# Last block's gate logits formed early, and the rows of the two last blocks placed by one-hot products

## The chip, the cores and the metric

One core of a Trainium2 chip runs the whole program. The metric is the device time of one execution in microseconds (us). Engines are named as in the profile: PE (TensorE, matrix products), PEld (its weight loads), DVE (VectorE), ACT (ScalarE), POOL (GpSimd) and SP (SyncE, which issues most DMAs).

## The reference, cut to what matters

```python
# 1. gated linear attention, step by step over 768 tokens, 2 batches x 8 heads x 40
m_new = max(f_t + m, i_t);  C = exp(f_t + m - m_new) * C + exp(i_t - m_new) * outer(v_t, k_t)
y_t = sigmoid(o_t) * (C @ q_t) / max(abs(n @ q_t), 1)
x = y as [1536, 320]
# 2. a dense layer pair, 2048 features
g = softplus(x @ w_in);   x2 = g @ w_out
# 3. eight experts, the best one for each token
logits = x2 @ w_gate;     e = argmax(logits);   p = softmax(logits)[e]
out = p * sigmoid(x2 @ w_output_gate)[e] * (relu(x2 @ w1[e]) @ w2[e])
```

Everything is float32. Where a product has to be exact enough for the argmax, an operand is split in a rounded high part and the rest (`xh`/`xl`, `gh`/`gl`, `part` 0 and 1), and several products are added.

## The kernel before

The 1536 tokens are six blocks of 256 (two tiles of 128, `t` = 0 and 1). Attention runs chunk by chunk (`chunk`, six chunks of 128 for both batches), and block `c` of stage 2 can begin when chunk `c` of both batches is done.

Stage 2: `up1` makes `ph`, the products of feature tile `f` (16 of them) with a block, eight 256-column products each. `softplus` (line 1188) turns `ph` into `g`: three ACT passes over `ab`, a DVE pass that writes `g`, an ACT copy `gh`, a DVE subtraction `gl`. `down1` (line 1239) adds `gh`, `gl` times `w_out` into `acc`. The features come in legs (0 to 4, 4 to 8, 8 to 16); the sum of a leg that isn't the last is kept in `row` by `keep_part`, and the last leg's sum is added to it by `take_row`.

Routing: when a block's last `acc` is full, `take_row` (line 874) writes `row`, turns it on PE (`x2tp`), copies it (`x2T`) and multiplies by `wg`, which holds both gates (`lg`). `route` finds the expert of each token (a DVE chain that ends in the one-hot `ohb`), PE counts how many tokens of an expert stand ahead (products with `tri` and `ones`), and a second DVE chain works out each token's place (`pos`). `scatter` sends the rows to the DRAM table `rows` by indirect DMAs from POOL. Stage 3 works on 15 slots of 128 places, each of one expert. The first four slots (`EARLY`) are needed at once, so `early_turn` (line 1124) builds their turned rows `xe` on PE: it transposes what blocks 0 to 4 have put there (`er`, read back from `rows`), and adds block 5's rows by products of `part` with `S`, the one-hot matrix of the places. `early_x` splits `xe` into the high and low half in `flat`, and the products `ph<-w1s,flat` of stage 3 begin.

Order: `Weaver` plans the program before it runs. Each engine has one queue that is worked off in the order in which the planner wrote it; the planner picks the next step by the start that its own price list gives, and by rank. A step that is priced too cheaply stands in the queue all the same, and what is behind it waits. `constants` (line 840) clears the routing tables on POOL and sends `wg` and the clearing of `rows` (19 DMAs); it comes up when 2, and then 12, up products are planned. `heat` (line 382) keeps PE busy until the gates have come in. `warm` (line 1151, called at 1477 to 1480) puts 14 idle products of 512 columns between the steps of the change-over to stage 3.

```python
W.add(warm(known, 5), 0)
W.add(warm(turned_rows[0], 2), 0)
W.add(warm(have_last_lg, 2), 0)
W.add(warm(have_turned, 5), 0)
```

Nearly all instructions of the trace have the line of a helper (L196), so steps are found by the names of their tiles.

Of the kernel before, what the change touches and what calls it, by code (L numbers as in the profile page):

```python
# [22 lines left out]
HEAT = 50  # L23
EARLY = 4
P = 128
# [209 lines left out]
def mlstm_moe_kernel(ctx: ExitStack, tc: tile.TileContext, q_t, k_t, k, v, i_gate, f_gate, o_gate,  # L235
# [16 lines left out]
    TPB = B  # L252
# [95 lines left out]
    scratch_all = moe.tile([P, (3 + NSP) * P + P // 2], F32, tag="row2", name="scratch")  # L348
    after_t = scratch_all[:, (3 + NSP) * P:].bitcast(BF16)
# [32 lines left out]
    def heat():  # L382
        warm, ev = yield from bank.get([P, 2 * P], F32, "heat")
        W.clock["P"] = 1.1
        yield "P"
        for _ in range(HEAT):
            PE.matmul(warm, ones, ones.unsqueeze(1).to_broadcast([P, 2, P]), start=True, stop=True)
        W.clock["P"] = 8.1
        W.signal(ev)

    def gates(n, c0, c1):
# [397 lines left out]
    def conv():  # L789
        for n in range(NF):  # L790
# [3 lines left out]
            t, e2 = yield from flt_ring.get([P, HIGH], U32, "wta", users=2)  # L794
# [8 lines left out]
            W.add(after(W.cur.out, low_p(t, e2, n)), 2)  # L803

# [6 lines left out]
    def low_p(t, ev, n):  # L811
        yield "G"
        psub(place(n)[64:P, 0:P], t[64:P, 0:P], place(n)[64:P, 0:P].bitcast(F32))
        W.signal(ev)
        W.signal(have_w[n])

# [23 lines left out]
    def constants():  # L840
        yield 2.0
# [17 lines left out]
        yield 12.0  # L859
# [14 lines left out]
    def take_row(row, t, acc, ev, part, xT, xT_ev, lg, lg_ev, eng, last):  # L874
        if part is not None:
# [5 lines left out]
            if last:  # L881
                W.add(after(W.cur.out, parts_of(row, t)), 2)
        else:
            yield eng
            copy(row[:, t, 0:DM], acc)
            copy(row[:, t, DM:CCOL], acc[:, 256:DM])
        W.signal(ev)
        xp, ev = yield from bank.get([P, 3, P], F32, "x2tp")
# [3 lines left out]
        if last:  # L892
            turned_rows[t].t = W.cur.out
        yield eng
        copy(xT, xp)
        W.signal(ev)
        if last:
            yield [turned_rows[TPB - 1]]
# [6 lines left out]
    def route(blk, acc, full, part):  # L905
# [9 lines left out]
        yield [full[0]]  # L915
        lg, ev = yield from bank.get([P, 64], F32, "lg")
        have_lg = Event(n=TPB)
        for t in range(TPB):
            xT, xT_ev = yield from xT_ring.get([P, 3, P], F32, "x2T")
            W.add(after(full[t], take_row(row, t, *acc[t], part, xT, xT_ev, lg, have_lg,  # L920
                                         "AV"[t % 2] if blk == NBLK - 1 else "A", blk == NBLK - 1)), 1)
        yield [have_lg]
# [10 lines left out]
        final = blk == NBLK - 1  # L933
        counts, counts_ev = (yield from bank_y.get([P, 64], F32, "counts")) if final else (lg, None)
        lgv = lg[:, 0:2 * T8].rearrange("p (t c) -> p t c", t=T2)
        le, lo_ = lgv[:, :, 0:E], lgv[:, :, E:2 * E]
        rank = counts[:, 2 * T8:3 * T8].rearrange("p (t e) -> p t e", e=E)
        tot = counts[:, 3 * T8:3 * T8 + E]
# [11 lines left out]
        tt(ohb, over(iota8, T2), bc(idx, E), ALU.is_equal)  # L950
        yield "P"
# [8 lines left out]
        yield "V"  # L960
        DVE.tensor_scalar(out=nmx, in0=mx, scalar1=-1.0, scalar2=None, op0=ALU.mult)
        tt(sel, lo_, ohb, ALU.mult)
        yield "V"
        DVE.tensor_reduce(out=oge, in_=sel, axis=AX.X, op=ALU.add)
        yield "A"
        for t in range(T2):
            ACT.activation(out=ex[:, t], in_=le[:, t], func=AF.Exp, bias=nmx[:, t:t + 1], accum_out=ssum[:, t:t + 1])
        ACT.activation(out=ef, in_=oge, func=AF.Exp, scale=-1.0)
        if final:
            W.signal(have_exps)  # L970
        yield [Event(ranked), state[blk], have_rows]
        if final:
            yield from place_last(small, tot, rank, ohb, ef, ssum, row, row_ev, ev, counts_ev, small_ev, blk)
            return
# [5 lines left out]
        yield from pause(blk)  # L980
# [21 lines left out]
        yield from pause(blk)  # L1002
        tt(t8, an, dn, ALU.mult)
        tt(c1, csi, rem.to_broadcast([P, E]), ALU.is_le)
        tt(room, room, tot, ALU.subtract)
        tt(c2, an, bn, ALU.add)
        yield from pause(blk)
        tt(nxt, nxt, t8, ALU.add)
        DVE.tensor_reduce(out=nmx[:, 0:1], in_=c1, axis=AX.X, op=ALU.add)
        tt(nmx[:, 1:2], total, rem, ALU.is_gt)  # L1010
        DVE.scalar_tensor_tensor(out=room, in0=c2, scalar=float(P), in1=room, op0=ALU.mult, op1=ALU.add)
        DVE.scalar_tensor_tensor(out=s128, in0=total, scalar=float(P), in1=s128, op0=ALU.mult, op1=ALU.add)
        yield from pause(blk)
        tt(nxt, nxt, tot, ALU.add)
        DVE.scalar_tensor_tensor(out=nmx[:, 1:2], in0=rem, scalar=0.0, in1=nmx[:, 1:2], op0=ALU.is_ge, op1=ALU.mult)
        W.signal(ev)
        yield from pause(blk)
        DVE.scalar_tensor_tensor(out=base, in0=room, scalar=s128, in1=nxt, op0=ALU.subtract, op1=ALU.add)
        DVE.scalar_tensor_tensor(out=esl, in0=nmx[:, 0:1], scalar=nmx[:, 1:2], in1=esl, op0=ALU.mult, op1=ALU.add)
        tt(rem, rem, total, ALU.subtract)  # L1020
        W.signal(small_ev)
        W.signal(state[blk + 1])
# [5 lines left out]
    def place_last(small, tot, rank, ohb, ef, ssum, row, row_ev, ev, counts_ev, small_ev, blk):  # L1028
# [17 lines left out]
        DVE.tensor_scalar(out=ef, in0=ef, scalar1=1.0, scalar2=None, op0=ALU.add)  # L1046
        yield "V"
        tt(m, m, over(dn, T2), ALU.mult)
        DVE.scalar_tensor_tensor(out=ef, in0=ssum, scalar=1e-9, in1=ef, op0=ALU.add, op1=ALU.mult)
        yield "V"  # L1050
        tt(nr, nr, m, ALU.add)
        DVE.reciprocal(out=row[:, :, CCOL], in_=ef)
# [8 lines left out]
        for t in range(T2):  # L1061
            W.add(after(placed, scatter(blk * TPB + t, row[:, t, :], posi[:, t:t + 1], row_ev)), 0)
        for t in range(T2):
            yield "V"
            DVE.tensor_scalar(out=chosen["S"][:, t], in0=chosen["iota"], scalar1=pos[:, t:t + 1], scalar2=None,
                              op0=ALU.is_equal)
        W.signal(have_chosen)
# [9 lines left out]
        for e in (ev, counts_ev, small_ev, state[blk + 1]):  # L1077
            W.signal(e)

    have_room, up_done, have_turned, have_exps, known = (Event() for _ in range(5))  # L1080
    have_last_lg, have_counts, have_chosen, have_parts, have_early = Event(), Event(), Event(), Event(n=TPB), Event()
    scattered_most = Event(n=NTILE - TPB)
    chosen, later = {}, {}
    x_done = Event(n=3)
# [12 lines left out]
    def early_rows():  # L1097
        yield [state[NBLK - 2]]
        for part in range(2):
            chosen["part", part], chosen["part_ev", part] = yield from row_ring.get([P, TPB, CCOL], F32R, "part")  # L1100
        W.signal(have_room)
# [4 lines left out]
        for n in range(EARLY // 2):  # L1106
            chosen["er", n], chosen["er_ev", n] = yield from raw_ring.get([P, 2, CCOL], F32, "er")
        chosen["S"], chosen["S_ev"] = yield from raw_ring.get([P, TPB, EARLY * P], F32R, "S")
# [6 lines left out]
    def parts_of(row, t):  # L1115
        yield [have_room]
# [657 lines left out]
```

## Time and profile before

| | |
|---|---|
| median of 3 runs | 435.1 us (434.52 to 436.67) |
| profiled execution | 435.17 us, of which 433.5 us are the span of the trace |
| PE busy | 410.1 us (95%), 3078 matrix products |
| DVE busy | 343.5 us (79%) |
| ACT busy | 302.5 us (70%) |
| POOL busy | 181.0 us (42%) |
| mean granted PE clock | 0.987 of full speed |

The span has three parts: attention, with stage 2 beginning among it, to about 130 us; stage 2 alone to about 278 us; stage 3 from about 294 us on. Between the last two stands the change-over. A busy share says how full an engine is over a stretch; what a stretch costs is read from the idle time of PE there and from the engine that ended it.

### The profile page before, as it was taken

Reading aid. Unit: us, or ns where it says so; the run is one execution under the profiler, and the core shown is the slowest. Engines: PE = TensorE matmul, PEld = TensorE weight load, DVE = VectorE, ACT = ScalarE, POOL = GpSimd, SP = SyncE. Lnnn points to the kernel's source line nnn. Section 1 sums busy time; section 2 is a strip of 40 time slices with the busy share of each in tenths; the row PEclk is TensorE's granted clock in tenths of the full one; section 3 lists DMA queues with packets and bytes.
Section 4 is the critical chain, followed back from the end, with each engine's and each line's share of the span. In section 5 each row is a group of like instructions: output and inputs, shape, how many; then the busy total and the mean of one; then the engine's idle time right before and its main releaser. Section 6 shows DMA issues by size and latency. Waiting matters only on the chain. (4 is left out here: it accounts for less than half of the span.)

```text
span 433.5 us, 9833 instructions
## 1 busy us (share of the span) xinstructions
PE 410.1 (95%) x3078; PEld 390.5 (90%) x3078; DVE 343.5 (79%) x904; ACT 302.5 (70%) x879; POOL 181.0 (42%) x246
## 2 busy tenths in 40 slices
PE   8877999999899999999999999899999999999994
PEld 6767999999899999999999999767998998998893
DVE  4999798998999999997657675666755898798663
ACT  2776699996868877777769669466798666566230
POOL 4256756756120111120201102127676287387654
PEclk9999899999999999999999999989999999999998
DMA  8958789499226412032101100128645636544112
GB/s 263 312 175 247 240 240 300 136 332 297 77 102 252 170 69 67 33 91 62 38 2 38 38 2 37 38 102 271 228 132 185 220 132 216 189 144 139 42 67 80
DMA packets 32284, 62.90 MB, mean 145 GB/s; under 512 B 4218, under 2 KB 16765, under 8 KB 32230
## 3 DMA queue, kind: packets, MB, share of 16 engines
q1 hardware_dynamic: 30742, 57.87, 41.0%
q0 software_dynamic: 1488, 4.35, 2.7%
q8 instruction: 28, 0.46, 0.4%
q14 instruction: 26, 0.21, 0.2%
HBM read 54.05 MB, written 8.65 MB: 145 GB/s over the span
## 5 line engine op out<-in xcount | busy, mean ns | idle before, releaser
L196 ACT ACTIVATE ab<-ab 128x256 f32<-128x256 f32 x192 | 77.4, 416 | 2.8
L196 PE MATMUL ph<-w1s,flat 128*128 x312 | 58.8, 332 | 2.6 <-DVE hr L196 1.5
L196 POOL TENSOR_TENSOR w1s<-w1raw,w1s 64x256 fp32r<-64x256 f32 (+1 forms) x39 | 39.4, 1027 | 48.5 <-ACT w1s L196 25.0
L196 PE MATMUL acc<-win,gh 128*128 128x320 f32 x240 | 56.1, 320 | 0.0
L196 DVE SCALAR_TENSOR_TENSOR g<-ph,ab 128x256 f32<-128x256 f32 x96 | 39.9, 419 | 20.2 <-ACT ab L196 19.5
L196 PE MATMUL yp<-w2s,hh 128*128 x240 | 54.6, 315 | 1.0 <-POOL w2s L196 0.9
L196 ACT ACTIVATE ab<-ph 128x256 f32<-128x256 f32 x96 | 36.0, 379 | 26.4 <-PE ph L196 26.2
L196 PEld LDWEIGHTS ph<-w1s,flat 128*128 128x128 f32 x312 | 46.6, 189 | 7.9 <-DVE hr L196 1.9
L196 DVE TENSOR_TENSOR gl<-g,gh 128x256 fp32r<-128x256 f32 x96 | 42.5, 447 | 7.9 <-ACT gh L196 7.2
L196 POOL DMA_INDIRECT rows<-row,rsm x12 | 12.0, 1004 | 80.4 <-DVE rsm L196 47.6
L196 POOL TENSOR_TENSOR w2s<-w2raw,w2s 128x640 fp32r<-128x640 f32 x22 | 39.1, 1808 | 8.7 <-issue 4.9
L196 ACT CAST gh<-g 128x256 fp32r<-128x256 f32 x96 | 38.1, 398 | 6.6 <-DVE g L196 4.7
L196 PEld LDWEIGHTS yp<-w2s,hh 128*128 128x128 f32 x240 | 39.8, 188 | 3.1 <-POOL w2s L196 1.1
L196 PE MATMUL ph<-win 128*128 128x256 f32 x250 | 40.8, 286 | 0.0
L196 DVE TENSOR_TENSOR hr<-ph,hr 128x256 f32<-128x256 f32 x60 | 24.7, 420 | 20.3 <-ACT hr L196 17.2
L196 PEld LDWEIGHTS acc<-win,gh 128*128 128x128 f32 x240 | 39.4, 191 | 0.0
L196 ACT COPY hr<-ph 128x256 f32<-128x256 f32 x60 | 22.6, 376 | 21.3 <-PE ph L196 19.2
L196 PE MATMUL acc<-win,gl 128*128 128x320 f32 x120 | 37.4, 312 | 0.0
L196 PE MATMUL yp<-w2s,hl 128*128 x120 | 37.2, 310 | 0.0
L196 PEld LDWEIGHTS ph<-win 128*128 128x128 f32 x250 | 34.3, 190 | 0.0
L196 PE MATMUL acc<-wou,gh 128*128 128x320 f32 x144 | 33.1, 315 | 1.2 <-ACT gh L196 1.2
L196 ACT CAST w2s<-w2raw 128x640 fp32r<-128x640 f32 x32 | 22.6, 735 | 13.9 <-PE yp L196 13.9
(209 smaller groups left out, 1070.6 us busy)
## 6 DMA issues: line engine op xcount, KB each, us to landing
w1raw<-in_w_dram SPq DMA_DIRECT2D x32, 384.0 KB, 4.4
wra<-in_w_in_dram SPq DMA_DIRECT2D x16, 704.0 KB, 5.1
w2raw<-in_w_dram SPq DMA_DIRECT2D x32, 320.0 KB, 3.2
abc<-abc_dram SPq DMA_DIRECT2D x4, 1024.0 KB, 7.8
rows<-pad SPq DMA_DIRECT2D x19, 194.0 KB, 4.4
qT<-in_q_t_dram SPq DMA_DIRECT2D x6, 512.0 KB, 4.4
kn<-in_k_dram SPq DMA_DIRECT2D x5, 416.0 KB
vn<-in_v_dram SPq DMA_DIRECT2D x6, 320.0 KB, 5.6
```

The lines of the kernel that those rows point to most:

```text
L196: return fn(*args, **kw)
```

## The change

- `heat` has 44 products in place of 50. The subtraction `ig - mm` on DVE is gone: PE adds minus `mm` to the turned `ig` by a product with a negative identity (`minus`).
- `constants` comes up at 20 and 26 planned up products in place of 2 and 12.
- The last block's last leg is cut in two: features 8 to 13, and 14 and 15 (`TAIL`). After the first of these the kept `row` is turned and multiplied by `wg` (`first_logits`, `part_logits`). For the two last features `vg` = `w_out` times `wg` is made once (`last_gates`), and the missing logits are `g` times `vg`, four products of 16 columns into the same `lg`. The `row` itself is finished later (`last_row`), behind the one-hot.
- Rows of block 4, too, are placed by one-hot products, so the read of `er` waits for blocks 0 to 3 alone. `xe` lies otherwise in its three banks: two banks hold two slots of two thirds each, one holds the last third of four slots. All products of high parts come ahead of those of low parts. A block takes 16 products of 256 columns and 4 of 512 (before: 12 of 512).
- The four calls of `warm` are gone. Scatters of the last block wait for the finished `row` and its weight.

```diff
-HEAT = 50
+HEAT = 44
+TAIL = 2
...
-        yield "V"
-        DVE.tensor_tensor(out=ig[:, t0:t1], in0=ig[:, t0:t1], in1=mm[:, t0:t1], op=ALU.subtract)
...
-            PE.transpose(gps[:, 1, c, :], ig[0:G, c * P:(c + 1) * P], ident[:G, :G])
+            PE.matmul(gps[:, 1, c, :], ig[0:G, c * P:(c + 1) * P], ident[:G, :G], start=True, stop=False, is_transpose=True)
+            PE.matmul(gps[:, 1, c, :], mm[0:G, c * P:(c + 1) * P], minus, start=False, stop=True)
...
+    def last_gates(t, ev, i):
...
+            PE.transpose(xp[0:n, kk, :], t[:, 3 * P + kk * P:3 * P + kk * P + n], ident)
...
+            PE.matmul(ps_, xT[0:n, kk, :], wg[0:n, kk, :], start=kk == 0, stop=kk == 2)
...
+        DVE.tensor_copy(out=vg[:, i], in_=ps_)
...
     def constants():
-        yield 2.0
+        yield 20.0
...
-        yield 12.0
+        yield 26.0
...
+    def first_logits(row, added):
+        yield [have_const, have_vg]
+        last["lg"] = lg, _ = yield from bank.get([P, 64], F32, "lg")
+        for t in range(TPB):
+            W.add(after(added[t], part_logits(row, t, lg)), 0.9)
+        yield [lg_parts, last_g]
+        for i in range(TAIL):
+            g, g_ev = last["g", i]
+            yield "P"
+            for t in range(TPB):
+                PE.matmul(lg[:, 2 * E * t:2 * E * (t + 1)], g[:, t * P:(t + 1) * P], vg[:, i], start=False,
+                          stop=t == TPB - 1 and i == TAIL - 1)
...
+    def last_row(row, t, acc, ev):
+        yield [turned_rows[t], have_ohb]
+        yield "V"
+        DVE.tensor_tensor(out=row[:, t, 0:DM], in0=acc, in1=row[:, t, 0:DM], op=ALU.add)
...
     def early_turn():
+        yield [have_early, known]
+        xe, half = [], EARLY // 2 * P
+        pieces = [[(0, 0, 2), (1, 0, 2)], [(2, 0, 4)], [(0, 2, 2), (1, 2, 2)]]
...
+        yield [have_chosen[LATE[0]], have_parts[LATE[0]]]
+        for n, group in enumerate(pieces):
+            for i in range(len(group)):
+                for part in range(2):
+                    for t in range(TPB):
+                        yield "P"
+                        product(n, i, LATE[0], t, part)
...
+        yield [have_chosen[LATE[1]], have_parts[LATE[1]]]
+        for part in range(2):
+            for n, group in enumerate(pieces):
...
+                        product(n, i, LATE[1], t, part, part == 1 and t == TPB - 1 and i == len(group) - 1)
...
+    legs[-1:] = [(NBLK - 1, cuts[-2], NF - TAIL), (NBLK - 1, NF - TAIL, NF)]
...
-    W.add(warm(known, 5), 0)
-    W.add(warm(turned_rows[0], 2), 0)
-    W.add(warm(have_last_lg, 2), 0)
-    W.add(warm(have_turned, 5), 0)
```

The planner writes another order from these. On POOL, in the attention part, the clearing of the routing tables stands before ahead of the product `v` that a chunk's state update (`kv` on PE) needs (`cst` is the state, `y` the chunk's result):

```order
L196 TENSOR_TENSOR cst_111<-cst_111,sm 40x4x41 x2
L196 MEMSET tri 128x128
L196 AFFINE_SELECT tri<-tri 128x128
L196 IOTA iota_115 128x8
L196 IOTA tokid 128x12
L196 MEMSET pad 128x388
...
L196 IOTA rem 128x1
L196 TENSOR_TENSOR v_575<-v_378,sm 128x328
```

and now:

```order
L197 TENSOR_TENSOR wou<-wta,wou 64x128 x2
L197 TENSOR_TENSOR y<-num,y 128x320
L197 MEMSET tri 128x128
L197 AFFINE_SELECT tri<-tri 128x128
L197 IOTA iota_120 128x8
...
L197 IOTA rem 128x1
L197 TENSOR_TENSOR y<-num,y 128x320
```

The fifteen small steps have moved from between the chunks to a place ahead of the last chunk's last result.

On PE, from the last up product of stage 2 to the places of the last block, the order before is this (`acc` are the last down products, `counts` the counting of tokens):

```order
L196 MATMUL ph<-xl,wou 128x256 x3
...
L196 MATMUL warm<-ones 128x512
L196 MATMUL acc_4141<-wou,gh 128x320 x2
...
L196 MATMUL x2tp<-ident,row 128x128 x3
L196 MATMUL lg<-wg,x2T 128x16 x6
L196 MATMUL xe_4396<-ident,er 128x128 x4
...
L196 MATMUL counts<-rsm,tri 128x8
...
L196 MATMUL xe_4398<-ident,er 128x128 x4
...
L196 MATMUL xe_4396<-S,part 128x512 x4
```

and now:

```order
L197 MATMUL x2tp<-ident,row 128x128 x6
L197 MATMUL ph<-xh,wou 128x256 x4
L197 MATMUL lg<-wg,x2T 128x16 x6
...
L197 MATMUL xe_4372<-ident,er 128x128 x4
L197 MATMUL acc_4285<-win,gh 128x320 x2
...
L197 MATMUL lg<-vg,g 128x16 x4
...
L197 MATMUL xe_4445<-ident,er 128x128 x4
L197 MATMUL xe_4372<-er,part 128x256 x8
...
L197 MATMUL xe_4372<-S,part 128x256 x4
```

The turning and the first logits have moved ahead of the end of the last up product, and the products of block 4 (`er` holds its one-hot matrix) stand between the counting and the products of block 5.

On DVE, before, the last block's softplus, rows and routing come in this order:

```order
L196 SCALAR_TENSOR_TENSOR g<-ph,ab 128x256
L196 TENSOR_TENSOR gl<-g,gh 128x256
L196 TENSOR_TENSOR row<-acc_4141,row 128x320
L196 TENSOR_TENSOR row<-acc_4177,row 128x320
L196 TENSOR_TENSOR part<-row,part 128x384 x2
L196 COPY x2T<-x2tp 128x384
L196 TENSOR_REDUCE rsm<-lg 128x2
```

and now:

```order
L197 TENSOR_TENSOR gl<-g,gh 128x256
L197 TENSOR_TENSOR nxt<-nxt,lg 128x8
L197 SCALAR_TENSOR_TENSOR rsm<-rem,rsm 128x1
L197 TENSOR_REDUCE rsm<-lg 128x2
L197 SCALAR_TENSOR_TENSOR base<-room,s_127,nxt 128x8
L197 SCALAR_TENSOR_TENSOR esl<-rsm,esl 128x1
L197 TENSOR_TENSOR rem<-rem,cum 128x1
```

The rows and their parts have moved behind the routing's first step; the bookkeeping of block 4 now lies around it, and `gl` still stands ahead of it.

## Rows read from the trace of the kernel before

**Rows 1.** Table by stretches: length, busy us of PE, PEld, DVE, ACT, POOL; clock; DMA

```profile
240.00:270.00 30.00, 30.00 (x244) 29.83 (x243) 19.17 (x99) 23.11 (x77) 4.73 (x8) 1.00 0.08 28
280.00:290.00 10.00, 9.04 (x51) 6.31 (x52) 7.11 (x36) 5.14 (x15) 0.49 (x1) 0.83 0.29 99
300.00:350.00 50.00, 49.60 (x346) 46.45 (x345) 34.62 (x76) 40.07 (x98) 27.57 (x39) 1.00 0.57 191
```

**Rows 2.** Timeline, attention part: start, length, step, count, idle time before and releaser

```profile
1.14 7.97 PE L196 MATMUL heat<-ones 128*128 128x256 bf16 x50 [1.14 <-DVE ones L196]
...
8.34 0.29 DVE L196 TENSOR_TENSOR ig<-ig,mm 80x128 f32<-80x128 f32 x1
...
40.00 1.21 POOL L196 TENSOR_SCALAR_AFFINE_SELECT tri<-tri 128x128 bf16<-128x128 bf16 x1
...
43.26 1.47 PE L196 MATMUL kv<-v,kn 128*104 128x82 f32 x8 [2.17 <-POOL v L196]
...
53.83 0.42 DVE L196 SCALAR_TENSOR_TENSOR g<-ph,ab 128x256 f32<-128x256 f32 x1 [2.57 <-ACT ab L196]
```

**Rows 3.** Table by stretches of PE alone: length, busy us, granted clock, DMA

```profile
44.00:45.00 1.00, 1.00 (x7) 0.50 1.04 405
...
286.00:287.00 1.00, 1.00 (x8) 0.50 0.00 0
```

**Rows 4.** Timeline of PE in stage 2: logits, turning, down products

```profile
268.68 0.73 PE L196 MATMUL lg<-wg,x2T 128*128 128x16 f32 x6
269.26 0.53 PE L196 MATMUL x2tp<-ident,row 128*128 128x128 f32 x3
269.55 0.54 PE L196 MATMUL acc<-wou,gh 128*128 128x320 f32 x2
...
270.07 0.45 PE L196 MATMUL acc<-wou,gh 128*128 128x320 f32 x2
270.36 0.31 PE L196 MATMUL acc<-wou,gl 128*128 128x320 f32 x1
270.51 0.46 PE L196 MATMUL acc<-wou,gh 128*128 128x320 f32 x2
```

**Rows 5.** Timeline of PE in the change-over

```profile
276.69 0.74 PE L196 MATMUL ph<-xh,wou 128*128 128x256 f32 x5
...
277.63 1.26 PE L196 MATMUL warm<-ones 128*128 128x512 bf16 x5
280.05 0.57 PE L196 MATMUL acc<-wou,gh 128*128 128x320 f32 x2 [1.17 <-ACT gh L196]
...
286.61 0.21 PE L196 MATMUL counts<-rsm,tri 128*128 128x8 bf16 x1
...
288.53 1.61 PE L196 MATMUL warm<-ones 128*128 128x512 bf16 x5
289.80 3.16 PE L196 MATMUL xe<-S,part 128*128 128x512 f32 x12
292.79 0.27 PE L196 MATMUL esp<-ident,esl 128*1 128x128 f32 x1
...
293.82 3.98 PE L196 MATMUL ph<-w1s,flat 128*128 x24 [0.65 <-DVE pad L196]
```

**Rows 6.** Timeline of DVE in the change-over

```profile
279.13 0.42 DVE L196 SCALAR_TENSOR_TENSOR g<-ph,ab 128x256 f32<-128x256 f32 x1 [1.40 <-ACT ab L196]
280.03 0.42 DVE L196 TENSOR_TENSOR gl<-g,gh 128x256 fp32r<-128x256 f32 x1 [0.47 <-ACT gh L196]
...
285.26 0.17 DVE L196 TENSOR_REDUCE rsm<-lg 128x2 f32<-128x16 f32 x1 [0.93 <-PE lg L196]
...
286.97 0.17 DVE L196 TENSOR_TENSOR newp<-counts,room 128x8 f32<-128x8 f32 x1 [0.30 <-PE counts L196]
...
288.57 0.87 DVE L196 TENSOR_SCALAR S<-iota,rsm 128x512 fp32r<-128x512 f32 x2
```

**Rows 7.** Timeline of ACT in the change-over: the copy of the turned rows

```profile
282.38 0.47 ACT L196 COPY x2T<-x2tp 128x384 f32<-128x384 f32 x1
```

More of the change, by code (lines that the diff above doesn't have):

```diff
@@ L880, in take_row @@
             copy(row[:, t, DM:CCOL], row[:, t, 256:DM])
-            if last:
-                W.add(after(W.cur.out, parts_of(row, t)), 2)
         else:
-            yield eng
+            yield "A"
             copy(row[:, t, 0:DM], acc)
@@ L887, in take_row @@
         W.signal(ev)
+        if blk == LATE[0]:
+            W.add(after(W.cur.out, parts_of(row, t, blk)), 2)
         xp, ev = yield from bank.get([P, 3, P], F32, "x2tp")
@@ L914, in route @@
         DVE.tensor_copy(out=row[:, :, CCOL + 1], in_=tokid[:, blk])
[L915 to L922, printed above, removed]
+        final = blk == NBLK - 1
+        if final:
+            for t in range(TPB):
+                W.add(after(full[t], last_row(row, t, *acc[t])), 1)
+            yield [have_lg_last]
+            lg, ev = last["lg"]
+        else:
+            yield [full[0]]
+            lg, ev = yield from bank.get([P, 64], F32, "lg")
+            have_lg = Event(n=TPB)
+            for t in range(TPB):
+                xT, xT_ev = yield from xT_ring.get([P, 3, P], F32, "x2T")
+                W.add(after(full[t], take_row(blk, row, t, *acc[t], part, xT, xT_ev, lg, have_lg)), ranks[blk])
+            yield [have_lg]
         T2, T8 = TPB, TPB * E
@@ L1012, in route @@
[L1012 to L1019, printed above, removed]
@@ L1024, in pause @@
+        if blk == NBLK - 2:
+            W.add(after(placed, book()), 1.5)
+        else:
+            yield from book()
     def pause(blk):
@@ L1138, in early_turn @@
-        W.mark(have_turned)
-        yield [have_chosen, have_parts]
-        for kk in range(3):
-            yield "P"
-            for t in range(TPB):
-                for part in range(2):
-                    PE.matmul(xe[kk][0], chosen["part", part][:, t, kk * P:(kk + 1) * P], chosen["S"][:, t], start=False,
-                              stop=t == TPB - 1 and part == 1)
-            W.add(after(W.cur.out, early_x(kk, *xe[kk])), 0)
+        W.cur.rank = 0
+        yield [have_chosen[LATE[1]], have_parts[LATE[1]]]
@@ new lines, in early_turn @@
+        for part in range(2):
+            for n, group in enumerate(pieces):
+                yield "P"
+                for i in range(len(group)):
+                    for t in range(TPB):
+                        product(n, i, LATE[1], t, part, part == 1 and t == TPB - 1 and i == len(group) - 1)
+                if part:
+                    for i, (kk, s, slots) in enumerate(group):
+                        for at in range(0, slots, 2):
+                            to = i * half + at * P
+                            W.add(after(W.cur.out, early_x(kk, s + at, xe[n][0][:, to:to + 2 * P], xe[n][1])), 0)
+            yield have_lows
@@ L1228, in up1 @@
                 W.signal(used_w[f])
-                W.add(after(W.cur.out, softplus(blk, f, ph, hev)), 1)
+                W.add(after(W.cur.out, softplus(blk, f, ph, hev)), 0.4 if blk == NBLK - 1 and f >= NF - TAIL else 1)
             if f1 == NF:
@@ L1260, in down1 @@
                         if f1 < NF:
-                            W.add(after(W.cur.out, keep_part(*acc[t], parts[blk], t, before)), 1)
+                            W.add(after(W.cur.out, keep_part(*acc[t], parts[blk], t, before)), 1 if f1 < NF - TAIL else 0.3)
                         else:
@@ L1266, in down1 @@
                 W.signal(used_w[f])
-                if f == NF - 2:
-                    W.add(route(blk, acc, full, parts.get(blk)), 1)
+                if f == NF - 2 and f0 == cuts[-2]:
+                    W.add(route(blk, acc, full, parts.get(blk)), ranks[blk])
         W.signal(down_done)
@@ L1442, in get_experts @@
         yield [ready]
-        esp, ev = yield from bank.get([1, 2 * P], F32, "esp")
+        esp, ev = yield from (bank_y if s1 == NS else bank).get([1, 2 * P], F32, "esp")
         yield "P"
```

276 lines of the change are left out of this document (194 added, 82 removed).

## The prediction

> **What bounds the kernel now.** I read first the table by stretches, then the timelines of PE, DVE and ACT around the places that the change touches. Through stage 2 and stage 3 PE is the engine that ends things: 30.00 of 30 us busy at 240 to 270, 49.60 of 50 at 300 to 350, with DVE, ACT and POOL well below [rows 1]. In these stretches a change is worth what it adds to or takes from PE's work. Two places are otherwise. In the change-over PE waits for a chain through ACT and DVE and back: the last up product starts at 276.69 and the first product of stage 3 at 293.82 [rows 5], 17.1 us later, and the granted clock between 280 and 290 is 0.83 in the mean [rows 1]. In the attention part PE stands for 2.17 us at 43.26, because the product `v` on POOL is late, then runs at 0.50, the 1.2 GHz level [rows 2, 3], and its lateness reaches DVE, which is idle for 2.57 us before 53.83 [rows 2]. The sum is made against the profiled execution's own 435.17 us (span 433.5 and 1.67 around it), which lies 0.07 above the median, so it needs no shift.
>
> **Start.** A heat product takes 7.97/50 = 0.159 us [rows 2], so six fewer free PE 0.95 us sooner. The subtraction on DVE (0.29 us from 8.34 [rows 2]) no longer stands ahead of the turned gates; the six small products that replace it lie on PE where it waits anyway. I take 0.9 us; nothing if DVE, which is full there, doesn't follow, 1.5 if the other subtractions count as well.
>
> **Constants.** The selection of `tri` alone takes 1.21 us on POOL, and the block of fifteen steps lasts from the memset ahead of it to `v`, which PE awaits. In the new order no `v` stands behind them. PE would get back the 2.17 us of waiting, and half of the some 3.4 us at 0.50 that follow (one slice of it is in [rows 3]): 3.9 us at most. But DVE is the engine that is full there, and it can be sooner only by what it lost, the 2.57 us before 53.83 [rows 2]. I take two thirds of that, 1.8 us, since the rest of the order there is new as well; the bounds are 0 and 2.9 us. From 60 us on PE is the bound, so what is won stays won. Start and constants together: 2.7 us, between 0 and 4.4.
>
> **The change-over, step by step.** I count from F, the point at which the last up product could start, 276.69 before [rows 5]. What moves F: six down products of feature 14 now come later, two times 0.44 us (270.07 to 270.51 [rows 4]), minus 0.88; new ahead of it are `last_gates`' two turnings, 0.29 us each (269.26 to 269.55), and two triples of gate products, 0.58 us for six (268.68 to 269.26) [rows 4], plus 1.16. So F is at 276.97, the win of the attention part left aside.
>
> Behind F come six turnings (0.58 us), six logit products (0.58) and the up product itself, 0.94 us (276.69 to 277.63 [rows 5]). The logits wait for two copies `x2T` of 0.47 us [rows 7], which ACT does one after the other between the passes of the softplus; I put 0.8 us of waiting to them. The up product ends at F + 2.9. From the end of an up product to the end of `g` it is 1.92 us and to the end of `gl` 2.82 us (277.63 to 279.55 and 280.45 [rows 5, 6]): `g` is there at F + 4.8, `gl` at F + 5.7. The products of `g` and `vg` are done at about F + 5.25, but DVE's first routing step stands behind `gl`, so it starts at F + 5.75 = 282.7. Before it started at 285.26 [rows 6]: 2.5 us won.
>
> From that step to the counting it was 1.35 us (285.26 to 286.61 [rows 5, 6]); with three steps of block 4's bookkeeping among it I take 1.45, F + 7.2. The down products that stand ahead of the counting, three groups of 0.44 us, have run by then. The place chain starts at F + 7.6, behind a row addition. It took 2.47 us with `S` (286.97 to 289.44 [rows 6]); with the second row addition and the weights among it I take 3.2: `S` is done at F + 10.8.
>
> PE meanwhile: counting to F + 7.5, five turnings at 0.1 us to F + 8.0, then block 4's 20 products. 256 columns take 0.94/8 = 0.1175 us, 512 columns 0.25 us (12 from 289.80 to 292.79) [rows 5]: 16 times 0.1175 and 4 times 0.25 is 2.9 us, so F + 10.9. That is where `S` is ready, too; the ten products of high parts hide the two subtractions of the low parts. Block 5's 20 products end at F + 13.8, and with the small `esp` products stage 3 begins at F + 14.1 = 291.1. The wait of 0.65 us for the cast `pad` [rows 5] goes, since `esp` has another bank now; the split of the first pieces is hidden by the products of the later ones. Before: 293.82. **Won: 2.75 us.** The 2.5 us of the chain thus stay, but not more, because PE has 2.9 us of products more to do and becomes the last. Doing block 4 there costs nothing only so long as DVE's chain lasts as long; its cover ends exactly at its end. Upwards the bound is 3.5 us (ACT's copies without waiting), downwards 1.1 us, if the clock falls once as it did (3.2 us at half, one slice at 286 to 287 in [rows 3], cost 1.6).
>
> Scatters, row loads and the splitting of `w2s` follow the places by the same distance as before, within half a microsecond, and PE in stage 3 is full [rows 1]; I put nothing there. The later clearing of `rows` lies in a stretch with little DMA traffic; nothing again.
>
> **Sum:** 435.17 - 2.7 - 2.75 = 429.7 us.
>
> **A rule that speaks against the change.** The rows show the clock at half at 286 to 287 [rows 3] although five warm products had been run from 277.63 on, and more followed [rows 5]. The Trainium skill, "TensorE: Matmul & The Clock Gate", Part 1, says that the slow level is the default and that activity releases it. By it, taking the warm products away would bring the slow level sooner or for longer; this is the second rival below. No run here shows the kernel without them.
>
> **Rivals.** First, **the attention part gives nothing**: POOL's block of constants is moved, not shortened, and at its new place, ahead of the last chunk's result, the next thing behind it waits in the same way, or DVE finds another wait. For it: DVE is nearly full there, and the order is new throughout. Against it: four groups of down products and three up products stand on PE between the two results that enclose the block. It leaves 435.17 - 2.75 = 432.4 us. [...]
>
> Second, **the clock is at half when the placing products begin**, and stays so through them. Without warm products PE waits for ACT and DVE from F + 3 to F + 7 with little between. It decides where PE enters the products at 1.2 GHz: 5.8 us of products and 0.5 us of turnings would take twice as long, 6.3 us more. For it: the clock fell in just this part before. Against it: down products of 320 columns now lie in the gap, and the products that follow are dense. With the whole 6.3 us and half of the win in the attention part it would be 435.17 - 1.35 - 2.75 + 6.3 = 437.4 us, slower than before.
>
> Third, **the chain isn't shortened**: ACT's copies, `gl` and the row additions that DVE has ahead of its steps take back what the early logits give, 2 us of the 2.75, beside a full win at the start: 435.17 - 2.7 - 0.75 = 431.7 us.
>
> **Chances.** Forecast 0.68, between 427.3 (both upper bounds: 4.4 and 3.5) and about 432; no win in the attention part 0.15, at 432.4; the chain not shortened 0.09, at 431.7; the slow clock 0.08, at 437.4. The range reaches from 427.3 to 433.6, which takes in the first rival with its lower bound of the change-over in part, and leaves out the slow clock and the upper end of the first rival. About 0.5% (2.2 us) is what a measurement can tell from no change: faster is below 432.9. The forecast and nearly all of the third rival are faster, and about half of the first; the rest of these and a mild case of the second are within it: faster 0.83, same 0.11, slower 0.06.
>
> **What would show it.** In the new profile: no wait of PE for POOL near 43 us and no half clock behind it; the first routing step of block 5 about 5.8 us behind the start of the turning that precedes the last up product; the products `xe<-er,part` ending when `S` is done, with no wait of PE at `xe<-S,part`; a clock of 1.00 through them; the first `ph<-w1s,flat` near 288.4. It would be wrong if PE waits anew in the attention part, if the first `xe<-S,part` waits for more than half a microsecond, or if stage 3 takes longer than the 139.7 us from 293.82 to the end.

## The result

The changed kernel takes 431.61 us in the median of 9 runs (429.8 to 432.93), the kernel before 434.98 (433.84 to 436.67) beside it: a ratio of 0.9914, 95% interval 0.9892 to 0.9936, some 3.4 us less by the medians and 3.7 by the ratio. 429.7 had been predicted. In a later series on one chip the ratio was 0.9935 (0.9909 to 0.9962). The profiled execution took 432.24 us, 430.5 of them its span, against 435.17 and 433.5.

| profiled execution, us | before | after | difference |
|---|---|---|---|
| F: last up product before; turning ahead of it after | 276.69 | 276.20 | -0.49 |
| first product of stage 3 | 293.82 | 289.99 | -3.83 |
| end of the span | 433.5 | 430.5 | -3.0 |

So 0.49 us were won ahead of F, 3.34 between F and stage 3, and 0.83 were lost in stage 3.

### The profile page after: what moved, and what is told of

Its sections match the earlier page's. It is cut to its first block, busy times and chain, and to the rows that moved or that the text cites. A ratio compares the mean times of both kernels' runs of the same rounds, so it can differ in the third digit from the quotient of the medians.

```text
span 430.5 us, 9934 instructions
## 1 busy us (share of the span) xinstructions
PE 411.9 (96%) x3124; PEld 394.8 (92%) x3124; DVE 340.7 (79%) x911; ACT 304.4 (71%) x891; POOL 181.9 (42%) x248
## 4 chain that ended last, share of the span: by engine, by line
PE 82%; DVE 6%; ACT 5%; issue 2%; POOL 2%; DMA 2%; SPq 0%; POOLq 0%; ACTq 0%; DVEq 0%
PE ph L197 29%; PE acc L197 20%; PE yp L197 12%; PE pv L197 5%; PE sp L197 3%; PE tp L197 3%; PE lg L197 2%; PE heat L197 2%; DMA yac<-rows 2%; PE qc L197 2%; DVE w2s L197 1%; PE xe L197 1%; ACT w2s L197 1%; PE kv L197 1%; PE x2tp L197 1%
## 5 line engine op out<-in xcount | busy, mean ns | idle before, releaser
L197 PE MATMUL ph<-w1s,flat 128*128 x312 | 61.2, 333 | 2.3 <-DVE hr L197 1.5
L197 POOL TENSOR_TENSOR w1s<-w1raw,w1s 64x256 fp32r<-64x256 f32 (+1 forms) x39 | 40.8, 1060 | 41.7 <-ACT w1s L197 24.0
L197 DVE TENSOR_TENSOR gl<-g,gh 128x256 fp32r<-128x256 f32 x96 | 41.1, 433 | 12.1 <-ACT gh L197 11.6
```

The lines of the kernel that those rows point to most:

```text
L197: return fn(*args, **kw)
```

## The profile after

PE in the change-over, as in [rows 5]: start, length, step, count, idle time before and releaser.

```profile
276.20 0.82 PE L197 MATMUL x2tp<-ident,row 128*128 128x128 f32 x6
276.78 0.72 PE L197 MATMUL ph<-xh,wou 128*128 128x256 f32 x4
277.34 1.45 PE L197 MATMUL lg<-wg,x2T 128*128 128x16 f32 x12
278.64 0.36 PE L197 MATMUL ph<-xh,wou 128*128 128x256 f32 x1
278.84 0.52 PE L197 MATMUL ph<-xl,wou 128*128 128x256 f32 x3
279.20 0.60 PE L197 MATMUL xe<-ident,er 128*128 128x128 f32 x4
...
283.39 0.17 PE L197 MATMUL lg<-rsm,tri 128*128 128x8 bf16 x1
...
284.02 3.07 PE L197 MATMUL xe<-er,part 128*128 128x256 f32 x20
286.93 3.08 PE L197 MATMUL xe<-S,part 128*128 128x256 f32 x20
289.85 0.27 PE L197 MATMUL esp<-ident,esl 128*1 128x128 f32 x1
```

The up product ends at F + 3.0, the counting is at F + 7.2, the products of block 4 end at F + 10.7 and those of block 5 follow with no wait. DVE over the same time, as in [rows 6]:

```profile
281.61 0.42 DVE L197 TENSOR_TENSOR gl<-g,gh 128x256 fp32r<-128x256 f32 x1
...
282.09 0.17 DVE L197 TENSOR_REDUCE rsm<-lg 128x2 f32<-128x16 f32 x1
...
283.70 0.17 DVE L197 TENSOR_TENSOR newp<-lg,room 128x8 f32<-128x8 f32 x1
...
286.06 0.88 DVE L197 TENSOR_SCALAR S<-iota,rsm 128x512 fp32r<-128x512 f32 x2
```

The first routing step stands behind `gl` and two small steps of block 4's bookkeeping, at F + 5.9, and `S` is done at F + 10.7, just as block 4's products end.

Ahead of F the picture is another. The table of PE alone (length, busy us, clock, DMA) for the two stretches up to F, before:

```profile
0.00:130.00 130.00, 119.05 (x976) 0.99 0.72 227
130.00:276.69 146.69, 146.69 (x1155) 1.00 0.19 66
```

and after:

```profile
0.00:130.00 130.00, 121.94 (x1003) 0.99 0.63 196
130.00:276.20 146.20, 146.20 (x1146) 1.00 0.31 100
```

All idle time lies ahead of 130 us. It fell from 10.95 to 8.06 us, by 2.89, about what was expected of the attention part. But PE's busy time up to F grew by 2.40 (265.74 to 268.14), and F came only 0.49 sooner. The added work is seen in two places of the timeline of PE, in a chunk's gates (first four rows) and in `last_gates` (the rest, once for each of two features):

```profile
29.29 0.21 PE L197 MATMUL gps<-ident,acum 16*128 16x16 f32 x1
29.35 0.21 PE L197 MATMUL gps<-ident,ig 16*128 16x16 f32 x1
29.41 0.37 PE L197 MATMUL gps<-scratch,mm 16*128 16x16 f32 x2
29.64 0.21 PE L197 MATMUL gps<-ident,acum 16*128 16x16 f32 x1
...
177.59 0.49 PE L197 MATMUL woT<-ident,wta 128*128 128x128 f32 x3
177.83 0.54 PE L197 MATMUL acc<-wou,gh 128*128 128x320 f32 x2
178.21 0.31 PE L197 MATMUL acc<-wou,gl 128*128 128x320 f32 x1
...
179.30 0.83 PE L197 MATMUL vgp<-wg,x2T 128*128 128x16 f32 x6
180.07 0.56 PE L197 MATMUL acc<-wou,gh 128*128 128x320 f32 x2
180.47 0.31 PE L197 MATMUL acc<-wou,gl 128*128 128x320 f32 x1
```

In `last_gates` the turnings take 0.24 us and the three gate products, which are six instructions, 0.77; the pair `acc<-wou,gh` behind each starts the next step 0.08 and 0.10 later than elsewhere (0.38 and 0.40 in place of 0.30). That is 1.19 us, and 2.4 for both features. A chunk's gates take 0.35 us (29.29 to 29.64), since the product with `minus` is two instructions. Before, a chunk's pair of turnings took 0.12. For six chunks that is 1.4 us more. With 0.6 less for `heat` (7.36 against 7.97) and 0.9 less for the moved down products, the sum is 2.3 of the measured 2.40.

## The experiments

All kernels were timed beside the kernel before on the same chip; "ratio" is to that. F stands for the start of the last up product, or of the turning that precedes it.

### The halves of the attention part

`b_const`: the two numbers of `constants`, 20 and 26, in the kernel before.

> The kernel before with one edit: the block of constants comes up at 20 and 26 planned up products in place of 2 and 12. Theory (the win of 1.8 us that the prediction gave to this step is there, and what hides it in the changed kernel is more work on PE): no wait of PE for POOL near 43 us, idle time of PE ahead of the last up product of stage 2 down from 10.95 us by 1.5 to 2, that product near 274.9 in place of 276.69, the whole near 433.2. Rival (the block is moved, not shortened; new waits take its place): that product within 0.5 of 276.69, the whole within 0.6 of the kernel before.

Measured: 435.12 us, ratio 1.0035 (1.0010 to 1.0061). There was no half clock in the whole attention part (3.4 us of it before), and yet the last up product ended only 0.5 us sooner (277.12 against 277.63).

`b_gates`: the start alone.

```diff
-HEAT = 50
+HEAT = 44
-        DVE.tensor_tensor(out=ig[:, t0:t1], in0=ig[:, t0:t1], in1=mm[:, t0:t1], op=ALU.subtract)
+            PE.matmul(gps[:, 1, c, :], mm[0:G, c * P:(c + 1) * P], minus, start=False, stop=True)
```

> The kernel before with the edits at the start alone: 44 heat products in place of 50, and minus mm added on PE in place of the subtraction on DVE. Theory (prediction): everything 0.9 us sooner, last up product of stage 2 at 275.8, the whole near 434.1. Rival, from the trace of the changed kernel, where the added product is two instructions and a chunk's gates take 0.36 us on PE against 0.12: PE does 1.4 us more for the gates and 0.6 less for the heat, so the product stays within 0.5 of 276.69, or is later by up to 0.8.

Measured: 435.68 us, ratio 1.0048 (1.0016 to 1.0080); F at 276.21. `b_heatconst` is `b_const` with 44 heat products as well, but with the subtraction on DVE. On PE its order up to the last up product is that of `b_const` without six heat products.

> The kernel before with 44 heat products and late constants, but with the subtraction on DVE as it was. It tells which of the two edits at the start goes with the late constants to give the 4 us that none of the halves gave. If the gain hangs on the subtraction leaving DVE: near the run with late constants alone, 0 to 2 us above the kernel before, with a stall of PE of over 1 us between 48 and 60 us. If it hangs on the order that the planner comes to, and the subtraction itself (0.29 us for the first chunk) is small: 3 to 4 us below the kernel before, last up product near 272.

Measured: 436.89 us, ratio 1.0034 (1.0002 to 1.0065). So neither half gains anything, nor does the late block with the shorter heat; each of these kernels is slightly slower than before. The late block with the minus product alone, at 50 heat products, was not tried.

### The whole attention part, and its complement

`b_att` is `b_const` and `b_gates` together. `a_back` is the changed kernel with all three edits undone.

> The kernel before with the whole attention part of the change (heat, minus product, late constants) and nothing else. Prediction: 2.7 us below the kernel before, with the last up product of stage 2 at 274.0 in place of 276.69. Rival, from the two runs of its halves, which were each 0.3 to 0.5% slower: the part gives nothing, the whole within 1 us of the kernel before or above it, and the gain of the change is made in the change-over.

> The changed kernel with its attention part undone (50 heat products, subtraction on DVE, constants at 2 and 12): the change-over alone. Prediction's term: 2.75 us below the kernel before. From the trace of the changed kernel: 3.8 won from the turning point to the first product of stage 3, 1.5 lost ahead of it (last_gates 2.4, less 0.9 for six down products moved), 0.8 lost in stage 3: 1.5 us below. If the attention part gives nothing: as fast as the changed kernel, 3.5 us below.

Measured: `b_att` 430.64 us, ratio 0.9923 (0.9887 to 0.9958); `a_back` 436.50, ratio 1.0038 (1.0013 to 1.0063). The attention part alone gives as much as the whole change, and the kernel with the change-over alone gains nothing. The rival for `b_att` is refuted. `b_att` differs from `b_heatconst` by the minus product alone (ratios 0.9923 and 1.0034): beside the late block, it is this edit that brings the gain. `a_back` is no clean removal, however: the planner put the turnings of the last block behind the last up product there (281.09 against 276.93), so the early logits came late, and stage 3 took 142.9 us.

Why the halves don't add up is seen in PE's stalls (idle time in brackets). `b_const`:

```profile
40.17 0.96 PE L196 MATMUL kv<-v,kn 128*104 128x82 f32 x8 [1.06 <-POOL v L196]
...
44.80 0.56 PE L196 MATMUL acc<-win,gh 128*128 128x320 f32 x2 [0.95 <-ACT gh L196]
...
53.63 0.56 PE L196 MATMUL kv<-v,kn 128*104 128x82 f32 x4 [1.55 <-issue]
```

`b_gates`:

```profile
39.35 0.96 PE L196 MATMUL kv<-v,kn 128*104 128x82 f32 x8 [1.38 <-POOL v L196]
...
42.32 0.56 PE L196 MATMUL acc<-win,gh 128*128 128x320 f32 x2 [1.08 <-ACT gh L196]
...
52.75 0.56 PE L196 MATMUL acc<-win,gh 128*128 128x320 f32 x2 [1.64 <-ACT gh L196]
```

`b_att`:

```profile
39.01 0.96 PE L196 MATMUL kv<-v,kn 128*104 128x82 f32 x8 [1.36 <-POOL v L196]
...
41.98 0.56 PE L196 MATMUL acc<-win,gh 128*128 128x320 f32 x2 [1.07 <-ACT gh L196]
```

All have the two stalls near 40. A third stall near 53 (in the kernel before, 1.11 us at 54.91) is gone only with both halves: PE is busy for 12.00 of 12 us from 48 to 60 in `b_att` and in the changed kernel. `b_heatconst` has it too (1.47 at 55.56). The late block and the minus product each make the planner write the whole attention part in another order; fewer heat products alone do not. The stall is some 1.6 of the 4.2 us by which the last up product ends sooner in `b_att` than in `b_const` (272.93 against 277.12, neither with a half clock); the rest was not traced to a step. Which step of that order removes the third stall was not isolated either.

### What the change-over costs ahead of F

`a_novg` leaves out `last_gates`: `vg` is set to zero by DVE, two features are missing from the last block's logits, and its tokens go to other experts in part.

> The changed kernel without last_gates: vg is set to zero by DVE, so two features are missing from the last block's logits, and its tokens go to other experts in part. It measures what last_gates costs. Theory, from the trace of the changed kernel (one last_gates is three turnings, 0.32 us, and twelve instructions over both for the gate products, 0.87 us each time): last up product of stage 2 some 2.4 us sooner, 273.8 against 276.20 for the product's turning point, the whole near 429.3. Rival (the prediction's 1.16 us): 275.0, the whole near 430.5. If other waits end last: no change.

Measured: 461.39 us, since the experts now need more slots than the 15 and a tail behind stage 3 runs; only the part up to F is read. F was at 271.65, 4.55 us sooner. Up to `last_gates` the orders are the same; the last step ahead of it, in this kernel

```profile
175.06 0.46 PE L197 MATMUL acc<-wou,gh 128*128 128x320 f32 x2
...
271.65 0.82 PE L197 MATMUL x2tp<-ident,row 128*128 128x128 f32 x6
```

stands at 177.15 in the changed one. So 2.09 us were there already (no half clock in this execution), and 2.46 us are `last_gates`: the 2.4 of the trace, not the prediction's 1.16. The eighteen instructions of `last_gates` are all that PE has less here up to F.

### Two executions of one program, and the half clock

`after2` is the changed kernel again.

> The changed kernel itself beside the others of this call, with a second trace of it. The order of its instructions is fixed, so what differs between the two traces is what executions differ by: I expect the stretch between 40 and 50 us to differ by up to 2 us at F (half clock there or not), and everything behind it to be a mere shift, the first product of stage 3 13.8 us behind F and 140.5 us from there to the end. Median 3.4 us below the kernel before.

Measured: 431.75 us, ratio 0.9935 (0.9909 to 0.9962); F at 275.11, stage 3 begins 13.8 us behind it and takes 141.1. The granted clock, one microsecond to a row, in the first trace of the changed kernel

```profile
44.00:45.00 1.00, 1.00 (x6) 0.50 1.00 406
```

and in the second:

```profile
32.00:33.00 1.00, 1.00 (x7) 0.50 0.94 363
...
44.00:45.00 1.00, 1.00 (x9) 1.00 0.99 396
```

The half clock had moved from 43 to 47 us to 31 to 35, with the same order of instructions. `a_hold` keeps PE at work in the two stalls near 40 with 18 idle products (ten are shown, eight more go into the bank of `kv`):

```diff
+                    if blk == 0 and f == 0 and t == 0:
+                        for _ in range(10):
+                            nc.tensor.matmul(acc[0][0][:, 0:2 * P], ones, ones..., start=True, stop=True)
```

> The changed kernel with 18 idle products of 256 bf16 columns in PE's two stalls near 38 and 42 us (8 into the bank of kv ahead of its real products, 10 into the bank of the first acc), written behind the planner's back so that the order stays. If the half clock between 43 and 47 us follows from PE standing still and costs about 2 us: the clock is 1.00 between 40 and 50, the turning point of the last up product lies near 274.2 in place of 276.20, the runs lie close together and the median is 1 to 1.5 us below the changed kernel's. If the clock falls for another reason: 0.5 remains in the trace and the median is the same, or later by the up to 2 us that the idle products take where PE does not wait.

Measured: 430.98 us, ratio 0.9917 (0.9886 to 0.9948), no half clock between 20 and 60, F at 274.35. That fits the first case in the trace, but it doesn't show a gain over `after2`: the intervals overlap. `v2` (below) has the same idle products and had the half clock from 30 to 37, ahead of the first of them at 40.95. And `b_att` and `a_novg`, which have the same order of PE there and none of the idle products, had no half clock either. So whether idle products keep it away is not shown.

### The end of the change-over

`b_nowarm`: the kernel before without its four calls of `warm`.

> The kernel before without its 14 warm products in the change-over. If they are what holds the clock up (the second rival of the prediction): the granted clock between 280 and 290 falls below 0.83, more of the placing products run at half, the first product of stage 3 comes 1 to 3 us behind 293.82, the whole at 436 to 438. If they only stand in the queue: the clock there is 0.83 or better, the first product of stage 3 is at 293.82 or up to 1 us sooner, the whole at 434.2 to 435.2.

Measured: 434.43 us, ratio 1.0018 (0.9988 to 1.0048), no difference that can be told. In the trace the clock did fall further, from 0.83 to 0.66:

```profile
280.00:290.00 10.00, 8.50 (x43) 0.66 0.24 79
```

and the first product of stage 3 came 17.6 us behind F in place of 17.1. The Trainium skill, "TensorE: Matmul & The Clock Gate", Part 1, says that the slow level is the default and activity releases it; the row agrees. Its price was half a microsecond: PE waits for DVE in this stretch in any case (0.41 us for `S`, 1.22 for `pad` in that trace).

`a_noblk4`: block 4's rows come back through `er` as in the kernel before, and its 20 products are left out; the output is the same.

```diff
-    scattered_most = Event(n=NTILE - 2 * TPB)
+    scattered_most = Event(n=NTILE - TPB)
...
-                        product(n, i, LATE[0], t, part)
```

> The changed kernel with block 4's rows read back from the table like those of blocks 0 to 3, so without its 20 one-hot products and with er waiting for its scatters. Prediction: the 2.9 us of products lie beside DVE's chain and cost nothing so long as that lasts as long; without them the placing products of block 5 start when S is done, F + 10.7, and the first product of stage 3 is at F + 13.8 as with them. If the read of er is the later one (block 4's second scatter starts 3.5 us behind F, lands 2.8 later, and the read takes 2 to 3): the turnings end up to 2 us behind S and the first product is at F + 14 to F + 16. If block 4's products held PE up: F + 13.3 or sooner.

Measured: 436.83 us, ratio 1.0032 (1.0003 to 1.0062).

```profile
276.77 0.82 PE L197 MATMUL x2tp<-ident,row 128*128 128x128 f32 x6
...
285.95 1.05 PE L197 MATMUL xe<-ident,er 128*128 128x128 f32 x4 [2.13 <-DMA er<-rows]
288.67 0.38 PE L197 MATMUL esp<-ident,esl 128*1 128x128 f32 x1 [1.66 <-DVE esl L197]
...
290.62 4.08 PE L197 MATMUL xe<-S,part 128*128 128x256 f32 x20
294.54 0.63 PE L197 MATMUL ph<-w1s,flat 128*128 x2
```

The read of `er` ends last, two small products stand ahead of the turnings and wait as well, and the placing runs partly at half clock (4.08 us against 3.08). Stage 3 begins at F + 17.8 in place of F + 13.8, worse than the F + 16 that I had as the late case. The early logits need block 4's products on PE: without them their gain is lost in a DMA.

`v1`: `b_att` with `esp` in another bank and three warm products in place of five ahead of the placing. `v2`: the same with the idle products of `a_hold`.

> The kernel before with the attention part of the change, and of the change-over only two small edits: the last esp takes one of the banks of the down sums (as in the changed kernel), and three warm products in place of five ahead of the placing products. In the trace with the attention part alone, PE starts the placing products 0.4 us behind S because of the warm products and waits 0.64 us for the cast pad ahead of stage 3. If PE is the bound there: first product of stage 3 16.4 us behind the start of the last up product in place of 17.4, stage 3 139.4 us as before, the whole 1 us below the attention part alone, some 5 us below the kernel before. If the rows that stage 3 reads back end it (theory): the first product 1 us sooner, but stage 3 0.5 to 1 us longer, and the whole within 0.5 of the attention part alone.

> As the run before this one, with the 18 idle products in PE's two stalls near 38 and 42 us. They had the clock at 1.00 between 40 and 60 us and the runs within 2.2 us of each other. Theory: the same here, single runs above 432 gone, the median 0.3 to 1 us lower than without them. Rival (the clock would have stayed up in this order anyway): the same median, or 0.2 later.

Measured: 431.76 us, ratio 0.9933 (0.9907 to 0.9959), and 431.33, ratio 0.9920 (0.9890 to 0.9950): no better than `b_att`; single runs above 432 us are still there in `v2` (up to 433.73). In `v1`:

```profile
288.62 1.44 PE L196 MATMUL ph<-w1s,flat 128*128 x5
290.55 3.21 PE L196 MATMUL ph<-w1s,flat 128*128 x19 [0.48 <-DVE pad L196]
...
294.03 0.82 PE L196 MATMUL xslot<-ident,yac 128*128 128x128 f32 x6
```

The first product of stage 3 came 15.7 us behind F in place of 17.4 (272.91 to 288.62; in `b_att` 271.97 to 289.39), but the wait for `pad` only moved behind it, and the rows read back (`xslot`) were turned 21.1 us behind F against 21.7. Stage 3 took 141.4 us against 139.4: all of the 1.7 us was given back. 0.85 us was lost behind the first `xslot`, with no single wait that shows it.

### Where the gain is, over the traces

Up to the step ahead of `last_gates` (177.15 in the changed kernel) PE's order is the same in the last eight kernels of this table, but for the idle products of `a_hold` and `v2`; the second column has the start of that step. `b_const` and `b_heatconst` are left out, since half of their last up product stands elsewhere, and `a_back` for its other order.

| | step ahead of `last_gates` | F | first product of stage 3 | F to the end | us at half clock, 20 to 60 |
|---|---|---|---|---|---|
| before | | 276.69 | 293.82 | 156.8 | 3.4 |
| `b_nowarm` | | 275.56 | 293.17 | 157.1 | 3.4 |
| `b_gates` | | 276.21 | 292.85 | 156.3 | 3.4 |
| `b_att` | 175.32 | 271.97 | 289.39 | 156.8 | 0 |
| `v1` | 176.26 | 272.91 | 288.62 | 157.1 | 3.4 |
| `v2` | 177.82 | 274.49 | 290.21 | 157.4 | 6.8 |
| `a_novg` | 175.06 | 271.65 | 285.36 | | 0 |
| after | 177.15 | 276.20 | 289.99 | 154.3 | 3.4 |
| `after2` | 176.08 | 275.11 | 288.91 | 154.9 | 3.4 |
| `a_hold` | 175.31 | 274.35 | 288.13 | 154.2 | 0 |
| `a_noblk4` | 177.75 | 276.77 | 294.54 | 159.1 | 6.8 |

From F to the end the new change-over is worth some 2.5 us (154.2 to 154.9 in three traces, 156.3 to 157.4 in six without it). What it costs ahead of F can be read without the spread of executions, between two instructions that all eight kernels have. In `b_att`:

```profile
175.32 0.45 PE L196 MATMUL acc<-wou,gh 128*128 128x320 f32 x2
...
271.97 0.76 PE L196 MATMUL ph<-xh,wou 128*128 128x256 f32 x5
```

From that step to F it is 96.6 to 96.7 us in the four kernels without `last_gates` and 99.0 to 99.1 in the four with it, and its eighteen instructions are all that differs there. So the change-over takes back 2.4 us ahead of F, all of it `last_gates`; the six down products that stand behind F now stand there in `b_att`, too. The attention part wins some 3 us: in traces with the same 3.4 us at half clock F lies at 275.6 to 276.7 with the kernel before, `b_nowarm` and `b_gates`, and at 272.9 with `v1`. What the change-over wins behind F it has paid ahead of it. Whether the changed kernel or `b_att` is the faster can't be told (ratios of one series 0.9935 and 0.9923, intervals overlapping), and no kernel here beats either.

## Why the prediction was right, and where not

The time lay 1.9 us above the forecast and within its range, the sign was right, and the span shows which terms failed. That it fell within the range is in part luck: of the two halves of the forecast gain, 2.7 and 2.75 us, the first came, and of the second next to nothing was left (2.5 won behind F, 2.4 paid ahead of it); a range of 6.3 us took that in. Two of the prediction's own signs of being wrong came true: PE waits anew in the attention part (1.56 us for `gh` at 42.73), and stage 3 takes longer than 139.7 us. The half clock behind 43 us, which was to go, was there in the first trace.

- **Start and constants, 2.7 us.** Right in size, wrong in its parts. The whole gives 0.9923 alone, and idle time ahead of F fell by 2.89. But 0.9 plus 1.8 is not how it comes about: neither half gained. Six heat products fewer freed 0.61 us (7.97 to 7.36), not 0.95: the mean of 0.159 us mixes slower products at the start (six to seven to a microsecond from 2 to 5 us) with faster ones (twelve from 6 to 8). Two thirds of 2.57 are 1.7, not 1.8. The reasoning from single waits named the POOL wait near 43 us, which is still there in small (1.36 us at 39.27 in the changed kernel); what went was PE's stall of 1.11 us at 54.91, which was not named; only DVE's idle time just ahead of it was (2.57 us before 53.83).
- **"The six small products that replace it lie on PE where it waits anyway."** Failed: they are twelve instructions in six groups and take 1.4 us of PE's time, not nothing.
- **`last_gates`, 1.16 us.** The step that failed most plainly. "0.58 us for six" was read as two triples of products; x6 in [rows 4] counts instructions (as do the 3078 "matrix products" of the table before), and a float32 product is two of them (the rounded operands, as in `acc`, take one). So six instructions are one triple. With the gaps behind it the term is 2.4. The 0.88 taken off for six down products was no gain of the change-over: in `b_gates` and `b_att` they stand behind F as well.
- **Behind F.** Right. 2.75 and 0.28 had been forecast between F and stage 3, 3.34 was measured; the up product at F + 3.0 (2.9 forecast), the routing step at 5.9 (5.75), the counting at 7.2 (7.2), `S` at 10.7 (10.8), block 4's products at 10.7 (10.9), stage 3 at 13.8 (14.1). The wait for `pad` [rows 5] is gone there, and the clock is 1.00 throughout. The twelve logit products, counted as six, fitted only because 0.8 us had been put to waits.
- **"Scatters, row loads ... follow the places by the same distance as before."** True, and the wrong distance to look at. POOL's second scatter of the last block starts at

```profile
290.79 0.98 POOL L196 DMA_INDIRECT rows<-row,rsm  x1 [0.30 <-issue]
```

before, and after at

```profile
288.55 0.97 POOL L197 DMA_INDIRECT rows<-row,rsm  x1 [0.30 <-ACT w2s L197]
```

It is 2.24 us sooner, while the first product of stage 3 is 3.83 sooner. The rows that stage 3 reads back therefore come 1.6 us later in its own time, and PE waits for them and for the copies of them:

```profile
295.99 1.19 PE L197 MATMUL ph<-w1s,flat 128*128 x6 [0.74 <-ACT flat L197]
...
299.86 0.85 PE L197 MATMUL xslot<-ident,yac 128*128 128x128 f32 x6 [0.33 <-DMA yac<-rows]
```

Before, there was one such wait of 0.42. Stage 3 took 140.51 us, 0.83 more, and 141.1 and 140.4 in the other two traces. `v1`, too, gave back an earlier first product, there in part to `pad`. Over the traces the two go together: where the second scatter starts 2.3 to 3.1 us ahead of the first product (before, `b_nowarm`, `b_gates`, `b_att`, `b_heatconst`), stage 3 takes 139.4 to 140.0 us; where it starts 1.4 to 1.5 ahead (the three traces of the new change-over, `v1`, `v2`), 140.4 to 141.7. `b_const` (1.8 ahead, 140.1) and `a_back` (0.9, 142.9) fall in line, `a_noblk4` does not (5.4, 141.4), and no run moved the scatter alone, so the cause is argued from the waits and not shown.

- **The rivals.** The first's 432.4 came close for another reason: the attention part gave its win, but `last_gates` spent what the change-over won. Its own mechanism did not come. The block of constants took 2.3 us at its new place (3.2 before), and behind it POOL stands idle, since the next step waits for DVE:

```profile
127.08 0.84 POOL L197 TENSOR_TENSOR y<-num,y 128x320 f32<-128x320 f32 x1 [2.18 <-DVE num L197]
```

The third's 431.7 is the measured time all but exactly, and is luck: the chain was shortened. The slow clock in the placing products did not come. `b_nowarm` lost half a microsecond in its trace with the old order, its placing products at full speed (3.09 us); in `a_noblk4`, where PE waits for the read of `er`, a part of them ran at half clock.

## What to carry to other kernels

Count what a profile's row counts: a float32 product stands as two instructions, so price a new step by instructions of the same kind, and add the step behind it. Work that is added early to shorten a later wait is only a gain if it costs less than it wins (here 2.4 us against 2.5), and if the next thing in line (here rows that go out and come back by DMA) moves by as much as the first product does. And where a planner orders the program, test the parts of a change alone and together: here the halves lost 0.35 and 0.5%, and both together gained 0.8%.

## What the runs showed of the hardware

The half clock in the attention part falls at another place in executions of the same program: 43 to 47 us in one trace of the changed kernel, 31 to 35 in the other. In kernels with the same order of PE there it lasted from 30 to 34 us (`v1`) or 30 to 37 (`a_noblk4`, `v2`), or did not come at all (`b_att`, `a_novg`, `a_hold`). In the five traces that have it PE is busy all the time while it lasts. Ahead of the fall near 43 stood a stall of 1.56 us. In `v1`, `a_noblk4` and `v2` the clock fell among gates products of 16 columns (28.9 to 30.8); in the first trace of the changed kernel no fall followed the same products (28.9 to 30.4).

Its price, too, differs by place. The step ahead of `last_gates` started at 175.1 to 175.3 us in the three traces without a half clock, at 176.1 and 176.3 with 3.4 us of it near 30, at 177.15 with 3.4 us near 43, and at 177.8 with 6.8 us. So 3.4 us at half clock cost about 1 us in one place and 1.9 in the other, and half of its length (1.7) is no safe estimate. `b_heatconst`, at half clock for 10.2 us from 31 to 42, ended the last up product 1.95 us behind `b_const`, which had none in the same order (and 0.6 us more of heat).

The kernel before and `b_nowarm` have the same order of PE's instructions up to the last up product and still reach it 1.13 us apart, with the same 3.4 us at half clock. The Trainium skill, "TensorE: Matmul & The Clock Gate", Part 1, tells of a spread between runs of one kernel in how long the clock is slow at its start; here the spread lies in mid kernel. Single executions of the kernel before went from 430.5 to 436.5 us in one series, so a single trace can't price a step of one microsecond unless the same instruction is compared at both its sides, as was done for `last_gates`.
